# Hashes on the full TensorE array, split operands for every head, and measured durations in a list scheduler

## The chip, the core and the metric

One core of a Trainium2 chip runs the whole program. The metric is device microseconds (us) of one execution. TensorE (PE) multiplies, VectorE (DVE), ScalarE (ACT) and GpSimd (POOL) do the elementwise work, and SyncE (SP) issues the DMAs.

## The reference, cut to what matters

Three stages, one after the other, on a batch of 2 sequences of 768 tokens with 8 heads of 64:

```python
q_bits = (einsum(q, proj) > 0)            # 6 hash bits a row, the same for k
mask = q_bucket[:, :, :, None] == k_bucket[:, :, None, :]
scores = where(mask, q @ k.T / 8, -1e9)   # attention within equal buckets
x = softmax(scores) @ v                   # -> 1536 x 512
h = ((x @ w1) * (x @ w2)) @ w3 @ w_out    # inner width 1024
out = (sigmoid(h @ w_gate) * (h @ w_val)) @ w_out2   # inner width 1536
```

Weights arrive as float64 and are decoded on the chip to float32. The products must hold float32 accuracy: a float32 value is split into a float32r high part and a float32r low part, and two or three float32r products stand for one float32 product.

## The kernel before, in words

**Attention** goes through 16 heads (`h`) of 6 row tiles (`g`, 96 in all). For a tile, `emit_qk` (L465, L468) puts 128 x 768 scores into one of two PSUM tiles, `emit_max` (L474, DVE) takes the row maximum, `emit_exp` (L484, ACT) the exponentials. For two tiles together (a unit, 48 in all) `emit_T` transposes on PE (L517) in three groups of four, copies each group out of PSUM on ACT (L520), and, for heads from `PLAIN = 2` on, writes the low part on DVE (L522). `emit_av` (L535) multiplies by v. For heads 0 and 1 it is six plain float32 matmuls with 64 columns of v as weights. For the other heads it is twelve float32r matmuls with 128 weight columns (high and low part of v side by side, made by `split_v` on POOL, L375 and L376), and `emit_x` then adds the two halves with one ACT copy and one DVE addition (L548). Plain heads need the ACT copy alone.

**The mask** rides in the score matmul: 64 extra contraction rows carry a pattern of the bucket. `hashes` makes them, twice a head: three matmuls with `pq` as weights (L388), the signs on ACT (L390), one matmul with the pattern `pat` (L391); DVE compares the result with a threshold (L413). DMAs on SP then move rows between partition halves.

**A filler** multiplies w3 by w_out (L590, 8 blocks of 24 matmuls) between the attention steps, each weight tile loaded by a 512 KB DMA and decoded by ACT, POOL and DVE (L337 to L346); afterwards the first quarter of the next stage takes its place. What follows attention, with three-part products at L695, runs to the end.

**The order** in the attention part is written by `order_engines`, which plays through all instructions with a cost for each (`cost`), a latency for each pair of engines and a landing time for each DMA, picks on each engine the ready instruction of highest priority, and then fixes that order on every engine and on SP's queue. Each engine works off its list in order: a wait at its head holds what is behind it.

Of the kernel before, what the change touches and what calls it, by code (L numbers as in the profile page):

```python
# [10 lines left out]
F32 = mybir.dt.float32  # L11
F32R = mybir.dt.float32r
U32 = mybir.dt.uint32
I32 = mybir.dt.int32
# [3 lines left out]
AF = mybir.ActivationFunctionType  # L18
# [10 lines left out]
class Tiles:  # L29
# [3 lines left out]
    rings = {}  # L33
# [12 lines left out]
def order_engines(tc):  # L46
# [8 lines left out]
    rings = Tiles.rings  # L55
    N = len(ins)

    def count(x):
        n = 1
        for _, c in list(x.ap)[1:]:  # L60
            n *= c
        return n
# [12 lines left out]
    def cost(k):  # L75
        i, e, op = ins[k], eng[k], type(ins[k]).__name__
        rd = [x for x in i.ins if hasattr(x, "ap")]
        n = max([count(i.outs[0])] + [count(x) for x in rd[:1]])
        if e == "PE":
            passes = 1 if "float32r" in str(rd[0].dtype) else 2 if n == 128 else 4  # L80
            return n / 2.4 * passes + 2.5
        if e == "Activation":
            return 971 if n == 768 else 50 + n * 0.836
        if e == "Pool":
            return 60 + n * 2.3
        if e == "DVE":
            if op in ("InstTensorTensor", "InstTensorReduce") or (op == "InstTensorScalarPtr" and len(rd) > 1 and count(rd[1]) > 8):
                return 69 + n * 1.04
            return 585 if op == "InstTensorScalarPtr" and n == 384 else 69 + n * 0.52
        return 600  # L90

    step = {("Activation", "DVE"): 145, ("Activation", "PE"): 200, ("Activation", "Pool"): 170, ("DVE", "Activation"): 132,
# [53 lines left out]
    def blocked(k):  # L146
        for t in opens.get(k, ()):
            g = rings[t][0]
            if slots[g] <= 0 or queue[g][taken[g]] != t:
                return g  # L150
            if g[0] == "mw" and pools.get("wtmp"):
                return "wtmp"
        return None
# [4 lines left out]
    dma = 0.0  # L158

    def wake(g):  # L160
        for k in waiting.pop(g, ()):
            heapq.heappush(ready[eng[k]], (ins[k].bass_priority, k))

    def post(t, what, x):
        heapq.heappush(events, (t, next(tick), what, x))
# [4 lines left out]
    while events:  # L170
        now = events[0][0]
        while events and events[0][0] <= now:
            _, _, what, x = heapq.heappop(events)
            if what == "ready":
                heapq.heappush(ready[eng[x]], (ins[x].bass_priority, x))
            elif what == "slot":
                g = rings[x][0]
                slots[g] += 1
                pools[g[0]] -= 1
                wake(g)  # L180
                if not pools[g[0]]:
                    wake(g[0])
            elif what == "end":
                for u in ends[x]:
                    left[u] -= 1
                    at[u] = max(at[u], now + step.get((eng[x], eng[u]), 60))
                    if not left[u]:
                        post(at[u], "ready", u)
                for t in held.get(x, ()):
                    todo[t] -= 1  # L190
                    if not todo[t]:
                        post(now + 200, "slot", t)
        again = True
        while again:
            again = False
            for e in ranks:
                while free[e] <= now and ready[e]:
                    _, k = heapq.heappop(ready[e])
                    g = blocked(k)
                    if g is not None:  # L200
                        waiting.setdefault(g, []).append(k)
                        continue
                    for t in opens.get(k, ()):
                        g = rings[t][0]
                        slots[g] -= 1
                        taken[g] += 1
                        if slots[g] > 0 and waiting.get(g):
                            wake(g)
                            again = True
                    order[e].append(k)  # L210
                    for u in begins[k]:
                        left[u] -= 1
                        at[u] = max(at[u], now)
                        if not left[u]:
                            post(at[u], "ready", u)
                    free[e] = done = now + cost(k)
                    if e == "SP":
                        n = count(ins[k].outs[0]) * list(ins[k].outs[0].ap)[0][1] * mybir.dt.size(ins[k].outs[0].dtype)
                        dma = max(now + 1080, dma) + n / 360
                        done = dma + 900  # L220
                    post(done, "end", k)
                    post(free[e], "free", k)
# [8 lines left out]
def lsh_attention_moe_moe2_kernel(  # L231
# [20 lines left out]
    B, H, S, D = v.shape  # L252
    P = 128
    NB = proj.shape[1]
    NT = S // P
    HS = S // 2
# [13 lines left out]
    act = nc.scalar  # L270
    dve = nc.vector
    pool = nc.gpsimd
    pe = nc.tensor
    sync = nc.sync

    def act_copy(dst, src):
        act.activation(out=dst, in_=src, func=AF.Copy)  # L277
# [4 lines left out]
    cst = Tiles(ctx.enter_context(tc.tile_pool(name="cst", bufs=1, side="left")), "cst", 1)  # L282
# [3 lines left out]
    psT = Tiles(ctx.enter_context(tc.tile_pool(name="psT", bufs=4, space=bass.MemoryType.PSUM)), "psT", 4)  # L286

    idf = cst.tile([P, P], F32, name="idf")
    pq_raw = cst.tile([P, NB], F32, name="pq_raw")
    pq = [cst.tile([P, D], F32R, name=f"pq{i}") for i in range(2)]  # L290
    thr = cst.tile([P, 2], F32, name="thr")
    scl = cst.tile([P, 1], F32, name="scl")
    zb = cst.tile([D, 1], F32, name="zb")
    pat = cst.tile([D, P], F32R, name="pat")
    bits = [cst.tile([D, P], I32, name=f"bits{i}") for i in range(2)]

    xall = big.tile([P, KC, NTOK], F32, name="xall")
    xraw = [xall[:, :, i * CH:(i + 1) * CH] for i in range(NSW)]
# [4 lines left out]
    psS = Tiles(att_ctx.enter_context(tc.tile_pool(name="psS", bufs=1, space=bass.MemoryType.PSUM)), "psS", 1)  # L303
    scs = [psS.tile([P, 2, 512], F32, name=f"s{i}") for i in range(2)]
    ap_ = Tiles(att_ctx.enter_context(tc.tile_pool(name="att", bufs=2, side="right")), "att", 2)
# [40 lines left out]
        dve.tensor_tensor(out=dst.bitcast(I32), in0=ai, in1=ri, op=ALU.add)  # L346


    PLAIN = 2

    raws, splits, mats = {}, {}, {}

    def load_v(h):
        if h < NH:
            if h < PLAIN:
                t = ap_.tile([P, 2, NT, D], F32, tag="spv", name=f"spv{h}")[:, 0]
# [13 lines left out]
    def split_v(h):  # L370
        if not PLAIN <= h < NH:
            return
        t = ap_.tile([P, NT, 2, D], F32R, tag="spv", name=f"spv{h}")
        splits[h, "v"] = t
        (pool if h >= 2 else dve).tensor_copy(t[:, :, 0, :], raws[h, "v"])  # L375
        pool.tensor_tensor(out=t[:, :, 1, :], in0=raws[h, "v"], in1=f(t[:, :, 0, :]), op=ALU.subtract)  # L376
# [6 lines left out]
    def hashes(m, half):  # L383

        hs = slice(half * HS, (half + 1) * HS)
        ps = psT.tile([P, 512], F32, tag="t", name="gps")
        for n, (w, x) in enumerate(((0, "aq"), (0, "bq"), (1, "aq"))):
            pe.matmul(ps[0:D, :HS], lhsT=pq[w], rhs=m[x][:, hs], start=n == 0, stop=n == 2)  # L388
        sg = ap_.tile([D, HS], F32R, tag="sg", name="sg")
        act.activation(out=sg, in_=ps[0:D, :HS], func=AF.Sign, scale=2.0 ** 64, bias=zb)  # L390
        pe.matmul(ps[:, :HS], lhsT=pat, rhs=sg, start=True, stop=True)  # L391
        return ps

# [30 lines left out]
    def first_head():  # L424
# [19 lines left out]
        for d in ("bk", "ak"):  # L444
            pool.tensor_copy(m[d][0:D], t[1][0:D])
        act_copy(m["bk"][D:P], f(m["bq"][D:P]))
        pss = [hashes(m, half) for half in range(2)]
        act.activation(out=m["bq"][D:P], in_=t[1][D:P], func=AF.Copy, scale=SCALE)
        for d, r in (("ak", slice(0, D)), ("aq", slice(D, P))):
# [59 lines left out]
    def emit_T(g, j):  # L509

        if g % 2 == 0 and j == 0:
            n, dt = (1, F32) if g < PLAIN * NT else (2, F32R)
            pt_t[g // 2] = [ap_.tile([P, 2, NT, P], dt, tag=f"pt{i}", name=f"pt{i}_{g}") for i in range(n)]
# [12 lines left out]
    def emit_av(u):  # L526
        pts = pt_t.pop(u)
        h, t = divmod(2 * u, NT)
        sv = raws[h, "v"] if h < PLAIN else splits[h, "v"].rearrange("p c a d -> p c (a d)")
        acc = psT.tile([P, 512], F32, tag="t", name=f"av{u}")  # L530
# [7 lines left out]
    def emit_x(u):  # L538
# [4 lines left out]
        x = xall[r0:r0 + D, hh // 2, b * S + t * P:b * S + (t + 2) * P]  # L543
        if h < PLAIN:
            act_copy(x, acc[0:D, :2 * P])
# [254 lines left out]
    start = first_head()  # L800
    next(start)
    make_identity(nc, idf)
    o = D // 2
    pool.iota(bits[0], pattern=[[0, 2], [1, D]], base=0, channel_multiplier=0)
    for r in range(0, D, o):
        pool.iota(bits[1][r:r + o], pattern=[[0, P]], base=0, channel_multiplier=1)
# [85 lines left out]
    for _ in first:  # L892
        pass
    order_engines(tc)
    prio(0, 200000)
    att_ctx.close()
# [44 lines left out]
```

## Time and profile before

| | |
|---|---|
| median of 3 runs | 832.86 us (831.72 to 833.24) |
| profiled execution, its own time | 831.98 us |
| its span, first to last instruction | 830.2 us |
| PE busy | 801.8 us, 97% of the span |
| ACT, DVE, POOL busy | 513.3, 458.0, 429.5 us |
| mean granted TensorE clock | 0.992 |

The span is what the rows cover; the profiled execution's time is 1.8 us longer. A busy PE counts from the start of a matmul to its modelled end, so the step from one start to the next says more about cost than a duration does.

### The profile page before, as it was taken

To read this page: it belongs to the slowest core of one execution; us is meant where nothing else is said; L and a number is where in the kernel's file an instruction comes from. 1 tells how busy PE (TensorE), PEld (TensorE's weight loads), DVE (VectorE), ACT (ScalarE), POOL (GpSimd) and SP (SyncE) were. 2 spreads that over 40 slices of the span, in tenths; PEclk is the share of its full clock that TensorE was granted. 3 is DMA by queue.
4 is the path that set the end of the run, shared out by engine and by line. 5 is a ranking of instruction groups with operands and counts; after the bars stand their busy time and mean duration, and the time that the engine had idled before them with its cause. 6 is when DMAs were issued, how large, how long until landed. Compare 5 with 4: busy or idle time off the path is not lost.

```text
span 830.2 us, 11487 instructions
## 1 busy us (share of the span) xinstructions
PE 801.8 (97%) x4016; PEld 657.1 (79%) x4016; DVE 458.0 (55%) x696; ACT 513.3 (62%) x944; POOL 429.5 (52%) x457
## 2 busy tenths in 40 slices
PE   5899899999999999999999999999999999999998
PEld 3577688888787888887888888888888888888886
DVE  5536787777788878977354535564522222222222
ACT  5788778787788888876455655766534333343332
POOL 5567656665466555559355556677633333333330
PEclk9999899999999999999999999999999999999999
DMA  8744547454455644131022122344001000010001
GB/s 259 199 153 129 171 125 188 130 156 112 121 147 145 147 102 128 61 137 51 1 74 79 52 77 76 103 152 135 17 1 51 1 1 1 0 52 1 0 1 51
DMA packets 28585, 74.46 MB, mean 90 GB/s; under 512 B 6128, under 2 KB 8432, under 8 KB 28528
## 3 DMA queue, kind: packets, MB, share of 16 engines
q1 hardware_dynamic: 28528, 73.73, 29.9%
q8 instruction: 32, 0.52, 0.3%
q14 instruction: 25, 0.20, 0.1%
HBM read 52.83 MB, written 3.19 MB: 67 GB/s over the span
## 4 chain that ended last, share of the span: by engine, by line
PE 86%; DVE 8%; ACT 3%; issue 1%; POOL 1%; DMA 0%; SPq 0%; DVEq 0%; POOLq 0%; ACTq 0%
PE m L695 18%; PE pa L695 17%; PE pb L695 17%; PE av L535 8%; PE tp L517 6%; PE wacc L590 5%; PE p L695 4%; PE s L465 3%; PE s L468 3%; DVE sm L474 2%; PE y L695 2%; PE gps L388 2%; DVE pt L522 2%; DVE da L341 1%; PE gps L391 1%
## 5 line engine op out<-in xcount | busy, mean ns | idle before, releaser
L735 DVE TENSOR_TENSOR pb<-pb,a 128x512 f32<-128x512 f32 x52 | 36.3, 699 | 179.0 <-PE pb L695 175.6
L474 DVE TENSOR_REDUCE sm<-s 128x1 f32<-128x768 f32 x96 | 91.0, 949 | 32.2 <-PE s L468 25.2
L689 POOL TENSOR_TENSOR wal<-xall,wah 128x512 fp32r<-128x512 f32 x36 | 46.9, 1304 | 107.2 <-ACT wah L277 107.2
L517 PE MATMUL tp<-idf,e 128*128 128x128 f32 x576 | 99.8, 278 | 1.0 <-DVE pt L522 1.0
L695 PE MATMUL pa<-x,wah 128*128 128x512 f32 x320 | 99.2, 390 | 0.0
L695 PE MATMUL pb<-x,wbh 128*128 128x512 f32 x320 | 98.6, 389 | 0.0
L520 ACT ACTIVATE pt<-tp 128x512 fp32r<-128x512 f32 (+1 forms) x144 | 82.8, 597 | 23.7 <-PE tp L517 22.6
L484 ACT ACTIVATE e<-s,sm 128x768 f32<-128x768 f32 x96 | 86.6, 902 | 13.8 <-DVE sm L474 12.4
L339 POOL TENSOR_SCALAR dr<-st 128x512 bf16<-128x512 f32 x76 | 71.0, 943 | 46.4 <-issue 25.7
L522 DVE TENSOR_TENSOR pt<-tp,pt 128x512 fp32r<-128x512 f32 x126 | 83.4, 683 | 18.1 <-ACT pt L520 17.7
L535 PE MATMUL av<-pt,spv 128*128 128x256 f32 (+1 forms) x576 | 86.0, 299 | 1.3 <-DVE pt L522 1.2
L517 PEld LDWEIGHTS tp<-idf,e 128*128 128x128 f32 x576 | 72.4, 143 | 12.5 <-issue 2.4
L535 PEld LDWEIGHTS av<-pt,spv 128*128 128x128 f32 (+1 forms) x576 | 73.7, 184 | 10.7 <-DVE pt L522 2.8
L590 PE MATMUL wacc<-wo,t 128*128 128x512 f32 x192 | 70.6, 434 | 6.3 <-ACT wo L277 2.8
L695 PEld LDWEIGHTS pa<-x,wah 128*128 128x128 f32 x320 | 60.1, 188 | 13.2
L695 PEld LDWEIGHTS pb<-x,wbh 128*128 128x128 f32 x320 | 60.1, 188 | 12.6
L465 PE MATMUL s<-bk,bq 128*128 128x384 f32 x192 | 61.8, 375 | 6.2 <-ACT e L484 5.7
L340 POOL TENSOR_SCALAR da<-da 128x512 f32<-128x512 f32 x76 | 48.3, 640 | 36.6 <-ACT da L337 32.5
L695 PE MATMUL pa<-x,wal 128*128 128x512 f32 x160 | 62.4, 391 | 0.9 <-POOL wal L689 0.9
L695 PE MATMUL pb<-x,wbl 128*128 128x512 f32 x160 | 62.5, 390 | 0.0
L468 PE MATMUL s<-ak,aq 128*128 128x384 f32 x192 | 60.2, 369 | 0.0
L338 ACT ACTIVATE dr<-st 128x512 int16<-128x512 uint32 x76 | 59.9, 788 | 0.0
(143 smaller groups left out, 1810.2 us busy)
## 6 DMA issues: line engine op xcount, KB each, us to landing
st<-in_moe_w_dram SPq DMA_DIRECT2D x32, 512.0 KB, 4.3
st<-in_moe_w_out_dram SPq DMA_DIRECT2D x20, 512.0 KB, 4.3
st<-in_moe_w_gate_dram SPq DMA_DIRECT2D x12, 512.0 KB, 3.2
st<-in_moe_w_val_dram SPq DMA_DIRECT2D x12, 512.0 KB, 3.2
qk<-in_qk_dram SPq DMA_DIRECT2D x15, 384.0 KB, 4.2
rr<-row SPq DMA_DIRECT2D x16, 192.0 KB, 3.5
out_dram<-o SPq DMA_DIRECT2D x12, 256.0 KB, 2.0
ak<-aq SPq DMA_DIRECT2D x15, 192.0 KB, 2.6
```

Source lines behind the costliest of these rows:

```text
L338: act.activation(out=r.bitcast(I16)[:, 0::2], in_=lw, func=AF.Copy, scale=2.0 ** -29)
L339: pool.tensor_scalar(out=r.bitcast(BF16)[:, 1::2], in0=f(hw), scalar1=0.0, scalar2=1.0, op0=ALU.mult, op1=ALU.mult)
L465: pe.matmul(s[:, half, :HS], lhsT=m["bq"][:, qs], rhs=m["bk"][:, ks], start=True, stop=False)
L468: pe.matmul(s[:, half, :HS], lhsT=m["aq"][:, qs], rhs=m["ak"][:, ks], start=False, stop=True)
L474: dve.tensor_reduce(out=b, in_=s[:, :, :HS], op=ALU.max, axis=AX.XY, negate=True)
L484: act.activation(out=e.rearrange("p (a c) -> p a c", a=2), in_=s[:, :, :HS], func=AF.Exp, bias=sm, scale=1.0, accum_out=su_t[h][:, t:t + 1],)
L517: pe.transpose(ps[:, i * P:(i + 1) * P], e_t[g - g % 2 + a][:, c * P:(c + 1) * P], idf)
L520: act.activation(out=dh, in_=src, func=AF.Copy)
L522: dve.tensor_tensor(out=d, in0=src, in1=f(dh), op=ALU.subtract)
L535: pe.matmul(acc[:w.shape[1], :2 * P].rearrange("p (a t) -> p a t", a=2), lhsT=w, rhs=r[:, :, c], start=(c == 0 and i == 0), stop=(c == NT ...
L590: pe.matmul(acc, lhsT=t3[x][:, j], rhs=wo[y][:, j], start=(j == 0 and n == 0), stop=(j == NF1 - 1 and n == 2))
L695: mm = pe.matmul(ps, lhsT=lhs[x], rhs=rhs[y], start=start and n == 0, stop=stop and n == 2)
```

## The change

The weights `pq` of the hash matmuls go from 64 to 128 columns (the added ones are zero), so the signs cover 128 rows, and `pat` has 128 rows (the added ones are zero). The scratch tiles `bits`, used once at the start, move into the ring of `ft`. `PLAIN` becomes 0, so heads 0 and 1 are split as all others are: their v goes through the single-buffered `rawv` and `split_v`, their transposed probabilities get a low part. In `order_engines` the costs of PE, ACT, POOL and DVE instructions and of DMA landings get other numbers; every engine's order in the attention part is made anew from them.

```diff
+        banks = [x for x in rd + [i.outs[0]] if (region(x) or ("",))[0] in rings and rings[region(x)[0]][0][0] in ("psT", "psS")]
         if e == "PE":
             passes = 1 if "float32r" in str(rd[0].dtype) else 2 if n == 128 else 4
-            return n / 2.4 * passes + 2.5
+            return n / 2.4 * passes + (16 if passes == 1 else -12 if passes == 2 else 4)
         if e == "Activation":
-            return 971 if n == 768 else 50 + n * 0.836
+            return 971 if n == 768 and banks else 50 + n * (0.836 if banks else 1.0)
         if e == "Pool":
-            return 60 + n * 2.3
+            if op == "InstTensorTensor":
+                return 40 + n * 2.4 if n < 768 else 2200
+            return 100 + n * 1.15
         if e == "DVE":
+            if op == "InstCustomDveAnt":
+                return 720
             if op in ("InstTensorTensor", "InstTensorReduce") or (...):
-                return 69 + n * 1.04
-            return 585 if op == "InstTensorScalarPtr" and n == 384 else 69 + n * 0.52
+                return 69 + n * (1.04 if banks else 1.4)
+            return 585 if op == "InstTensorScalarPtr" and n == 384 else 69 + n * 0.6
...
-                        dma = max(now + 1080, dma) + n / 360
+                        dma = max(now + 1900, dma) + n / 300
                         done = dma + 900
...
-    pq = [cst.tile([P, D], F32R, name=f"pq{i}") for i in range(2)]
+    pq = [cst.tile([P, P], F32R, name=f"pq{i}") for i in range(2)]
-    zb = cst.tile([D, 1], F32, name="zb")
-    pat = cst.tile([D, P], F32R, name="pat")
-    bits = [cst.tile([D, P], I32, name=f"bits{i}") for i in range(2)]
+    zb = cst.tile([P, 1], F32, name="zb")
+    pat = cst.tile([P, P], F32R, name="pat")
...
-    PLAIN = 2
+    PLAIN = 0
...
-            pe.matmul(ps[0:D, :HS], lhsT=pq[w], rhs=m[x][:, hs], start=n == 0, stop=n == 2)
-        sg = ap_.tile([D, HS], F32R, tag="sg", name="sg")
-        act.activation(out=sg, in_=ps[0:D, :HS], func=AF.Sign, scale=2.0 ** 64, bias=zb)
+            pe.matmul(ps[:, :HS], lhsT=pq[w], rhs=m[x][:, hs], start=n == 0, stop=n == 2)
+        sg = ap_.tile([P, HS], F32R, tag="sg", name="sg")
+        act.activation(out=sg, in_=ps[:, :HS], func=AF.Sign, scale=2.0 ** 64, bias=zb)
         pe.matmul(ps[:, :HS], lhsT=pat, rhs=sg, start=True, stop=True)
...
+    bits = ap_.tile([P, S], F32R, tag="ft", name="bits", bufs=1).bitcast(I32)
+    bits = [bits[0:D, i * P:(i + 1) * P] for i in range(2)]
```

## Rows read from the trace of the kernel before

**Rows 1.** Page, busy time and instructions of each engine
```profile
PE 801.8 (97%) x4016; PEld 657.1 (79%) x4016; DVE 458.0 (55%) x696; ACT 513.3 (62%) x944; POOL 429.5 (52%) x457
```

**Rows 2.** Stretches: length, busy time by engine (instructions), granted clock, DMA
```profile
20.00:80.00 60.00, 56.14 (x292) 40.16 (x291) 32.34 (x48) 47.88 (x94) 39.11 (x48) 0.96 0.56 160
...
90.00:100.00 10.00, 8.63 (x43) 7.39 (x44) 7.09 (x11) 7.21 (x15) 7.29 (x9) 0.66 0.31 101
...
100.00:380.00 280.00, 272.69 (x1677) 233.65 (x1676) 228.02 (x341) 227.14 (x448) 167.35 (x197) 1.00 0.48 131
220.00:240.00 20.00, 17.95 (x111) 14.74 (x111) 19.23 (x30) 17.34 (x36) 11.30 (x14) 1.00 0.47 134
260.00:280.00 20.00, 19.60 (x125) 16.96 (x125) 18.97 (x30) 16.86 (x33) 12.15 (x16) 1.00 0.56 163
...
500.00:600.00 100.00, 100.00 (x432) 80.72 (x431) 54.34 (x86) 66.20 (x111) 70.01 (x70) 1.00 0.30 100
```

**Rows 3.** Waits of PE: total us, times, longest us
```profile
PE gps L388 <- ACT aq L440: 6.7, 1, 6.7
PE s L465 <- ACT e L484: 5.7, 6, 1.4
PE wacc L590 <- ACT wo L277: 2.8, 1, 2.8
PE wacc L590 <- ACT t L277: 2.5, 3, 1.4
...
PE wacc L590 <- POOL wo L585: 0.9, 1, 0.9
```

**Rows 4.** Timeline of PE, one unit of head 1 and one of head 2
```profile
62.16 2.80 PE L535 MATMUL av<-pt,spv 128*64 128x256 f32 x12
64.89 0.50 PE L590 MATMUL wacc<-wo,t 128*128 128x512 f32 x1
...
82.80 1.58 PE L535 MATMUL av<-pt,spv 128*128 128x256 f32 x12
84.21 0.27 PE L517 MATMUL tp<-idf,e 128*128 128x128 f32 x1
```

**Rows 5.** Timeline of PE around one pattern matmul of the hashes
```profile
103.00 0.34 PE L388 MATMUL gps<-aq,pq 128*64 128x384 f32 x1
103.17 0.34 PE L468 MATMUL s<-ak,aq 128*128 128x384 f32 x1
103.35 0.39 PE L590 MATMUL wacc<-wo,t 128*128 128x512 f32 x1
103.67 0.44 PE L391 MATMUL gps<-sg,pat 64*128 64x384 f32 x1
104.04 0.44 PE L517 MATMUL tp<-idf,e 128*128 128x128 f32 x2
```

**Rows 6.** Timeline of PE's weight loads, the same pattern matmul
```profile
103.67 0.18 PEld L391 LDWEIGHTS gps<-sg,pat 64*128 64x128 f32 x1 [0.30 <-ACT sg L390]
```

**Rows 7.** Line L391: duration ns least, median, most; first and last start
```profile
L391 PE MATMUL gps<-sg,pat x32: 435/439/686, 9.9 to 322.4; 64*128 64x384 f32 x32
```

**Rows 8.** Groups of instructions by form: busy us, mean ns, idle before
```profile
L522 DVE TENSOR_TENSOR pt<-tp,pt 128x512 fp32r<-128x512 f32 x126 | 83.4, 683 | 18.1 <-ACT pt L520 17.7
L520 ACT ACTIVATE pt<-tp 128x512 fp32r<-128x512 f32 x126 | 72.5, 598 | 20.9 <-PE tp L517 19.7
L339 POOL TENSOR_SCALAR dr<-st 128x512 bf16<-128x512 f32 x76 | 71.0, 943 | 46.4 <-issue 25.7 <-DVE w1r L346 10.1 <-DVE wc L346 5.6
...
L390 ACT ACTIVATE sg<-gps,zb 64x384 fp32r<-64x384 f32 x32 | 17.8, 572 | 6.1 <-PE gps L388 5.7
L548 DVE TENSOR_TENSOR xall<-av,xall 64x256 f32<-64x256 f32 x42 | 17.4, 415 | 14.2 <-ACT xall L277 13.7
...
L376 POOL TENSOR_TENSOR spv<-rawv,spv 128x384 fp32r<-128x384 f32 x14 | 15.3, 1094 | 1.0
```

**Rows 9.** DMA issues: count, KB each, median us to landing
```profile
st<-in_moe_w_dram SPq DMA_DIRECT2D x32, 512.0 KB, 4.3
```

## The prediction

> **What bounds the kernel now.** I read the page first: PE is busy 801.8 of 830.2 us, no other engine above 513.3 [rows 1]. That is an average over two parts, so the stretches come next [rows 2]. Behind attention PE never rests (500 to 600 us: 100.00 busy), and the change touches nothing there. In attention, from 100 to 380 us, PE is busy 272.69 of 280, DVE 228.02 and ACT 227.14 (81% each). So attention is bound by PE too, but with two engines not far behind. An instruction taken off PE's list there shortens the run, as long as DVE and ACT can follow. The early stretch, 20 to 80 us, has PE at 56.14 of 60 and DVE at only 32.34. The waits of PE tell what is lost now [rows 3]: 6.7 us at the start for the first load, 5.7 for exponentials, and 2.8 + 2.5 + 0.9 = 6.2 us for operands of the filler, which PE's list held too early. Last I read the timeline for the steps from start to start, because durations overlap.
>
> **Plain float32 to split for heads 0 and 1.** A unit's product with v takes 64.89 - 62.16 = 2.73 us in plain float32 and 84.21 - 82.80 = 1.41 us split [rows 4]. Two heads have 2 x 6 / 2 = 6 units, so PE loses 6 x 1.32 = 8.0 us of work. In return DVE gets 6 x 3 low parts of 0.683 us (12.3 us), 6 additions of 0.415 (2.5) and 2 copies of v. The trace has no such copy on DVE; I bound it by 0 and by the 0.683 of a wider tile, and take the upper end, 1.4. Sum 16.2 us [rows 8]. POOL gets 2 subtractions of 1.094 us, which the 60 - 39.1 us it has free from 20 to 80 us hide; without that cover they cost 2.2 [rows 2, 8]. With the 8.0 us gone from the stretch, DVE has 32.3 + 16.2 = 48.5 us to do in 52, or 93%. The two fullest DVE stretches later show what that does to PE: at 19.23 of 20 PE idled 2.05 us, at 18.97 only 0.40 [rows 2]. Scaled to 52 us this is 1 to 5 us; I take the middle, 3 us lost. What would be late is the low part, and with it the next product with v on PE, and behind the DVE's subtraction the row maxima of the next tiles.
>
> The v of head 1 now waits until `split_v` has read head 0's, because the raw tile has one buffer. That load sits on SP's queue with the weight loads behind it. A weight load lands in 4.3 us [rows 9], so a misplaced v load would hold the decode by 0 to 4.3 us, once. The new order plans for this wait, so I take 0 and keep 4.3 as the bound.
>
> **The hashes on 128 rows.** The pattern matmul has 64 rows of weights now. Its weight load does not start until its own matmul does (both 103.67), where others run ahead [rows 5, 6]. Before it, a matmul of 512 columns takes 103.67 - 103.35 = 0.32 us. The normal step of that size is 100 us / 432 = 0.23 [rows 2], so 0.09 is lost. The step after it is 104.04 - 103.67 = 0.37, where a matmul of 384 columns on the full array steps by 103.35 - 103.17 = 0.18; I use the 0.17 of the neighbour at 103.00, so 0.20 is lost. Together 0.29 us. There are 32 of them with nearly one duration (435 least, 439 median) [rows 7]. The first two run in the start, where PE waits anyway; 30 x 0.29 = 8.7 us leaves PE.
>
> The Trainium skill, TensorEngine Tiling (Array Packing), Key Properties, says that changing the tiling mode drains TensorE. For 64 rows the trace agrees (0.29 us a visit). The page makes no exception for 64 columns, and there the trace disagrees: from the last hash matmul with 64 columns to the next with 128 the step is 0.17 us, as between equals [rows 5]. By the page the sum would be rival 5's, by the rows it stays.
>
> The wider hash weights cost nothing by the same steps: 0.17 with 64 columns, 0.18 with 128 [rows 5]. If the longer load of 128 columns showed, it would be 0.01 us x 96 = 1 us. The sign over 128 rows should not be longer than over 64: the ACT copy of 128 rows and 512 elements takes 598 ns, the sign of 64 rows and 384 takes 572, so 0 to 26 ns each, 0.8 us in all of an engine that is not the bound [rows 8]. The wider constants and the `bits` move are written while PE waits 6.7 us for its first operands [rows 3]; without that cover a few memsets remain, under 0.7 us together.
>
> Of the 8.7 us, 22 visits lie between 100 and 380 us (6.4 us). DVE then has 228 us in 273.6, 83%. The stretches at 95% lost 0.4 to 2.05 in 20; at 83% I expect a trace of that, 1 us in all.
>
> **The order.** A changed number costs no instruction; it moves waits. The largest corrections: a POOL tensor-scalar of 512 elements was planned as 60 + 512 x 2.3 = 1.24 us, now 0.69, and takes 0.943 in the mean [rows 8]. A 512 KB load was planned to land after 1.08 + 1.46 + 0.9 = 3.4 us, now 1.9 + 1.75 + 0.9 = 4.5, and lands after 4.3 [rows 9]. A load planned to land 0.9 us too early is just what puts a filler matmul at the head of PE's list before its operand is there. So the gain is bounded by the 6.2 us of filler waits [rows 3] plus the clock that dropped after them: 0.66 granted from 90 to 100 us, between the levels 1.2 and 2.4 GHz, 3.4 us lost [rows 2]. In the other direction, POOL is now planned 0.25 us too short, and new waits can appear anywhere; as a bound all 8 filler blocks wait as long as the worst one, 8 x 2.8 = 22.4, less the 6.2, so 16 us more. The corrected loads are nearest to the measured waits, so I take a gain of 3, half of the filler waits.
>
> **The sum**, against the profiled execution's 831.98 us (0.9 under the median, inside the runs shown): - 8.0 + 3 - 8.7 + 1 - 3 = - 15.7, which gives 816.3. I say 816.5, about 2% faster.
>
> **Rivals.**
> 1. DVE becomes the bound in heads 0 and 1 and the whole early saving goes: 93% planned load speaks for it, the filler that PE can do meanwhile against it. With no gain of the order either: 831.98 - 8.7 = 823.3. With the v load's 4.3 us on top, 827.6.
> 2. The order gives all it can: 831.98 - 8.0 - 8.7 - 6.2 - 3.4 + 4 = 809.7, and some of the 5.7 us of waits for exponentials lies beyond that, so down to 804.
> 3. Slower: PE's list holds the first matmul of each filler block before its weight is decoded, because POOL's decode is planned too short. The waits in [rows 3] show that such a wait reaches PE. It decides from 16.7 / 8 + 6.2 / 8 = 2.9 us a block, about the worst wait of now; with the clock dropping behind half of them (4 x 3.4 = 13.6) the time is 831.98 - 16.7 + 16.2 + 13.6 = 845. Against it: POOL's error shrinks from +0.3 to -0.25 us, and loads get more time.
> 4. The gap before the pattern matmul is a wait for the sign, not for the array: the load's idle time of 0.30 ends with ACT's sign [rows 6]. Then 30 x 0.09 = 2.7 us stay: 819. The 0.20 behind it can't be the sign's.
> 5. Entering and leaving a run of 64-column matmuls costs PE what the pattern matmul costs it. With one such run for each of the 30 pattern matmuls another 30 x 0.29 = 8.7 us goes: 816.3 - 8.7 = 807.6. The step of 0.17 us at 103.00 speaks against it [rows 5]. This is the rule of the Trainium skill's TensorEngine Tiling (Array Packing), Key Properties, applied to columns.
>
> **Chances.** The forecast, 811 to 822: 0.49; rival 4 inside it: 0.06; rival 1, 822 to 829: 0.17; rival 2, 804 to 811: 0.15; rival 5: 0.02; rival 3: 0.07; and a part of rival 3 that just cancels the gains: 0.04. Under 0.2% (1.7 us) a measurement of this kernel, whose three runs lie 1.5 us apart, can't tell a difference from none. Faster 0.89, same 0.04, slower 0.07. The range 806 to 829 leaves out the 0.11 above and some 0.07 of rival 2 below.
>
> **What the profile after would show.** No form 128*64 or 64*128; the pattern matmul stepping by 0.17 to 0.18 us with its weight load ahead of it; 48 units of av with about 1.4 us each. L522 with 144 instructions, L548 with 48. PE's waits for wacc under 6.2 us. DVE near 48 us in the first 75. The stage behind attention unchanged in length, only earlier. The forecast is wrong if PE's waits in attention grow by over 10 us, above all for DVE's low parts before 80 us, or if the granted clock stays low early.

## The result and the profile after

The changed kernel takes 813.48 us (median of 4 runs, 812.90 to 815.98) against 833.05 for the kernel before: a ratio of 0.9771 (95% interval 0.9745 to 0.9797), 19.6 us faster. The forecast was 816.5 in a range of 806 to 829. The total came out near; the terms behind it did not, and they are what the experiments are about.

The page of the changed kernel, busy time and instructions of each engine (compare [rows 1]):

```profile
PE 785.3 (97%) x4016; PEld 657.4 (81%) x4016; DVE 469.1 (58%) x722; ACT 512.2 (63%) x944; POOL 436.1 (54%) x459
```

PE does 16.5 us less and DVE 11.1 more; ACT's work is unchanged. The stretches of the changed kernel (columns as in [rows 2]):

```profile
20.00:80.00 60.00, 52.70 (x330) 44.97 (x330) 51.76 (x80) 53.40 (x107) 50.84 (x63) 1.00 0.70 190
20.00:100.00 80.00, 71.46 (x446) 60.86 (x447) 70.87 (x109) 71.85 (x142) 67.30 (x83) 1.00 0.73 196
...
380.00:800.00 420.00, 420.00 (x1824) 342.10 (x1823) 157.32 (x241) 200.92 (x338) 183.27 (x165) 1.00 0.13 43
```

Of the kernel before, the early and the late stretch:

```profile
20.00:100.00 80.00, 72.47 (x378) 53.62 (x378) 48.26 (x70) 62.91 (x123) 51.82 (x64) 0.93 0.56 161
...
380.00:800.00 420.00, 420.00 (x1825) 342.15 (x1824) 163.11 (x248) 204.40 (x345) 196.50 (x175) 1.00 0.13 44
```

Read the instruction counts in brackets. From 20 to 100 us PE is busy no longer than before (71.46 against 72.47) but gets 446 matmuls done instead of 378. ACT does 142 instructions instead of 123, DVE 109 instead of 70, the DMAs move 22% more a second, and the granted clock is 1.00 instead of 0.93. From 380 to 800 us PE is full in both, with 1824 and 1825 matmuls: that part moved forward and kept its length, as forecast.

PE's waits in the changed kernel (columns as in [rows 3]):

```profile
PE wacc L594 <- ACT wo L282: 2.9, 2, 2.0
...
PE wacc L594 <- ACT t L282: 0.6, 1, 0.6
...
PE wacc L594 <- POOL wo L589: 0.3, 1, 0.3
```

The filler's waits fell from 6.2 to 2.9 + 0.6 + 0.3 = 3.8 us, a small part of 19.6. These waits can't show how much work each engine's list (its fixed order of instructions) got through, and there the two kernels differ by more.

### The profile page after: what moved, and what is told of

It is laid out like the page before. It is cut to its first block, busy times and chain, and to the rows that moved or that the text cites. A ratio compares the mean times of both kernels' runs of the same rounds, so it can differ in the third digit from the quotient of the medians.

```text
span 810.8 us, 11521 instructions
## 1 busy us (share of the span) xinstructions
PE 785.3 (97%) x4016; PEld 657.4 (81%) x4016; DVE 469.1 (58%) x722; ACT 512.2 (63%) x944; POOL 436.1 (54%) x459
## 4 chain that ended last, share of the span: by engine, by line
PE 84%; DVE 7%; ACT 5%; POOL 2%; issue 1%; DMA 1%; SPq 0%; POOLq 0%; ACTq 0%; DVEq 0%
PE m L699 18%; PE pa L699 18%; PE pb L699 18%; PE av L539 6%; PE tp L521 5%; PE p L699 5%; PE wacc L594 4%; PE s L469 3%; PE s L472 3%; PE y L699 3%; DVE pt L526 2%; PE gps L392 2%; DVE sm L478 1%; ACT e L488 1%; ACT pt L524 1%
## 5 line engine op out<-in xcount | busy, mean ns | idle before, releaser
L526 DVE TENSOR_TENSOR pt<-tp,pt 128x512 fp32r<-128x512 f32 x144 | 94.9, 681 | 11.4 <-ACT pt L524 10.7
L343 POOL TENSOR_SCALAR dr<-st 128x512 bf16<-128x512 f32 x76 | 73.0, 970 | 41.1 <-issue 21.0
L488 ACT ACTIVATE e<-s,sm 128x768 f32<-128x768 f32 x96 | 86.7, 905 | 12.3 <-DVE sm L478 11.7
L524 ACT ACTIVATE pt<-tp 128x512 fp32r<-128x512 f32 x144 | 82.5, 600 | 11.0 <-PE tp L521 9.3
L539 PE MATMUL av<-pt,spv 128*128 128x256 f32 x576 | 77.2, 283 | 1.0 <-DVE pt L526 0.9
L539 PEld LDWEIGHTS av<-pt,spv 128*128 128x128 f32 x576 | 71.5, 188 | 5.8 <-DVE pt L526 4.1
L699 PEld LDWEIGHTS pa<-x,wah 128*128 128x128 f32 x320 | 60.1, 188 | 13.2
L594 PE MATMUL wacc<-wo,t 128*128 128x512 f32 x192 | 66.7, 418 | 3.7 <-ACT wo L282 2.9
L344 POOL TENSOR_SCALAR da<-da 128x512 f32<-128x512 f32 x76 | 50.1, 665 | 31.1 <-ACT da L341 26.7
```

Source lines behind the costliest of these rows:

```text
L343: pool.tensor_scalar(out=r.bitcast(BF16)[:, 1::2], in0=f(hw), scalar1=0.0, scalar2=1.0, op0=ALU.mult, op1=ALU.mult)
L488: act.activation(out=e.rearrange("p (a c) -> p a c", a=2), in_=s[:, :, :HS], func=AF.Exp, bias=sm, scale=1.0, accum_out=su_t[h][:, t:t + 1],)
L524: act.activation(out=dh, in_=src, func=AF.Copy)
L526: dve.tensor_tensor(out=d, in0=src, in1=f(dh), op=ALU.subtract)
L539: pe.matmul(acc[:w.shape[1], :2 * P].rearrange("p (a t) -> p a t", a=2), lhsT=w, rhs=r[:, :, c], start=(c == 0 and i == 0), stop=(c == NT ...
L594: pe.matmul(acc, lhsT=t3[x][:, j], rhs=wo[y][:, j], start=(j == 0 and n == 0), stop=(j == NF1 - 1 and n == 2))
```

## The experiments

All times are medians, with the ratio to the kernel before on the same chip where one is quoted. A gain in us that stands behind a ratio is worked out from it; a difference from the changed kernel is one of medians, and under some 2 us it is within the spread of the runs. Every run makes the order anew from its own instructions, so a small part of any difference can be the order's.

### Each part alone, and two without the third

The change has three parts that can be had one by one: hashes on 128 rows and columns, split heads 0 and 1, and the new numbers in `order_engines`. `hash_only`, `split_only` and `order_only` take the kernel before with one of them.

The edits are the lines of the change itself, and all of these kernels have the move of `bits`. In `hash_only`:

```diff
-    pq = [cst.tile([P, D], F32R, name=f"pq{i}") for i in range(2)]
+    pq = [cst.tile([P, P], F32R, name=f"pq{i}") for i in range(2)]
-    pat = cst.tile([D, P], F32R, name="pat")
+    pat = cst.tile([P, P], F32R, name="pat")
...
-        sg = ap_.tile([D, HS], F32R, tag="sg", name="sg")
+        sg = ap_.tile([P, HS], F32R, tag="sg", name="sg")
```

In `split_only`:

```diff
-    PLAIN = 2
+    PLAIN = 0
```

In `order_only` all new lines of `cost`, and:

```diff
-                        dma = max(now + 1080, dma) + n / 360
+                        dma = max(now + 1900, dma) + n / 300
```

`hash_split` has the first two edits and not the third.

> The kernel before with the hashes on 128 rows and columns alone; float32 heads 0 and 1 and the old costs stay. Theory 1 (the terms of the sum hold one by one): 8.7 us less PE work, about 1 given back, so 7 to 9 us under the kernel before, near 825. Theory 2 (the new order brings most, because a gain on PE is lost in the old order's waits): under 4 us, 829 or more. The pattern matmul should step by 0.17 to 0.18 us.

825.02 us, ratio 0.9912 (0.9895 to 0.9928): 7.3 us, as the sum said. PE's busy time falls from 801.8 to 793.1 us, by just the 8.7 us of the forecast.

> The kernel before with heads 0 and 1 split alone. Theory 1: 8.0 us less PE work, 3 lost to DVE, so about 5 us under the kernel before, near 828. Theory 3 (DVE becomes the bound in heads 0 and 1): within 2 us of the kernel before, with PE waiting on DVE's low parts before 80 us. Theory 2: within 4 us.

831.37 us, ratio 0.9987 (0.9978 to 0.9997): 1.1 us, where the sum said 5. By the pages PE is busy 7.1 us less (801.8 to 794.7), and idle 5.7 us more: the work is gone, and most of it came back as idle time.

> The kernel before with the new costs of the list scheduler alone. Theory 1: 3 us under the kernel before, near 830, with under 4 us of filler waits. Theory 2: 8 us or more under it, with the granted clock at 1.0 from 10 to 50 and from 90 to 100 us, where it was 0.66 to 0.93.

818.89 us, ratio 0.9841 (0.9826 to 0.9855): 13.2 us, where the sum said 3. The new order alone is worth more than both cuts of PE's work. The granted clock is 1.00 in every ten microseconds from 10 to 100 us, where the kernel before had 0.66 to 0.93 in five of the nine.

> The changed kernel with the old costs: both cuts of PE work, old order. Theory 1: 8.7 + 8.0 - 4 = 12.7 us under the kernel before, near 820, 4 to 7 us over the changed kernel. Theory 2: over 825, more than 11 us over the changed kernel.

824.62 us, ratio 0.9907 (0.9892 to 0.9922): with the old order both cuts together bring no more than the hashes alone, and the changed kernel lies 11.1 us below. This is theory 2 for the split (its 825 missed by 0.4) and theory 1 for the hashes.

`hash_order` is the changed kernel with heads 0 and 1 in plain float32 again:

```diff
-    PLAIN = 0
+    PLAIN = 2
```

> The changed kernel with float32 heads 0 and 1 (PLAIN = 2). Theory 1: 5 us over the changed kernel, near 818. Theory 3 (DVE takes the early saving): within 2 us of the changed kernel. If the gain of the split is its whole 8.0 us of PE work: 821.5.

815.32 us: the split brings 815.32 - 813.48 = 1.8 us in the new order, which is not clear of the spread (812.63 to 816.69 here, 812.90 to 815.98 in the changed kernel).

`split_order` is the changed kernel with the hashes on 64 rows and columns again (the diff of `hash_only` turned round).

> The changed kernel with the hashes on 64 rows and columns. Theory 1: 7 to 9 us over the changed kernel, 820 to 822. Theory 2 (order brings most): under 4 us over it.

817.32 us: the hashes bring 3.8 us in the new order, half of what they bring in the old one.

### Rows or columns

`cols_only` is the changed kernel with signs and pattern on 64 rows, the hash weights staying on 128 columns:

```diff
-    pat = cst.tile([P, P], F32R, name="pat")
+    pat = cst.tile([D, P], F32R, name="pat")
...
-        sg = ap_.tile([P, HS], F32R, tag="sg", name="sg")
-        act.activation(out=sg, in_=ps[:, :HS], func=AF.Sign, scale=2.0 ** 64, bias=zb)
+        sg = ap_.tile([D, HS], F32R, tag="sg", name="sg")
+        act.activation(out=sg, in_=ps[0:D, :HS], func=AF.Sign, scale=2.0 ** 64, bias=zb)
```

> The changed kernel with 128 columns in the hash weights, but signs and pattern over 64 rows as before. If the rows alone cost PE time (my reading of the trace): the pattern matmul again steps by 0.37 us, and the time is that of the kernel with both on 64, 7 to 9 us over the changed kernel. If leaving 64 columns costs as much as leaving 64 rows: the time lies between, and the changed kernel's gain from the hashes is about twice 8.7.

817.37 us, the time of the kernel with both on 64 (817.32).

`rows_only` is the changed kernel with the hash weights on 64 columns, signs and pattern staying on 128 rows; rows 64 to 127 of two fixed sign tiles are zeroed once:

```diff
-    pq = [cst.tile([P, P], F32R, name=f"pq{i}") for i in range(2)]
+    pq = [cst.tile([P, D], F32R, name=f"pq{i}") for i in range(2)]
+    sgs = [cst.tile([P, HS], F32R, name=f"sg{i}") for i in range(2)]
...
-            pe.matmul(ps[:, :HS], lhsT=pq[w], rhs=m[x][:, hs], start=n == 0, stop=n == 2)
-        sg = ap_.tile([P, HS], F32R, tag="sg", name="sg")
-        act.activation(out=sg, in_=ps[:, :HS], func=AF.Sign, scale=2.0 ** 64, bias=zb)
+            pe.matmul(ps[0:D, :HS], lhsT=pq[w], rhs=m[x][:, hs], start=n == 0, stop=n == 2)
+        sg = sgs[half]
+        act.activation(out=sg[0:D], in_=ps[0:D, :HS], func=AF.Sign, scale=2.0 ** 64, bias=zb)
...
+    for t in sgs:
+        dve.memset(f(t[D:P]), 0.0)
```

> The changed kernel with 64 columns in the hash weights, signs and pattern over 128 rows (the upper 64 rows of two fixed sign tiles are zero, ACT writes the lower 64). If the rows alone cost PE time: within 1 us of the changed kernel, the pattern matmul at 0.17 to 0.18 us. If columns cost as well: 4 us or more over it, with steps above 0.2 us out of the last hash matmul.

813.19 us, the time of the changed kernel (813.48). So the whole gain of the hashes comes from leaving the 64 rows; no cost of the 64 columns shows. Rival 5 is out. The Trainium skill's sentence that a change of the tiling mode drains TensorE (TensorEngine Tiling (Array Packing), Key Properties) fits what the 64 rows cost here (817.37 against 813.48), and no cost of that kind shows for the 64 columns. Whether the array drains at either was not shown.

### Does DVE hold the early stretch?

Both are the changed kernel without the low parts of the probabilities of two heads; PE multiplies the high part a second time in their place. DVE loses 18 subtractions, 12.3 us by [rows 8] (by the pages it is busy 8.9 and 10.3 us less), and PE keeps its work. `no_low_early` (in `no_low_late` the heads are 8 and 9):

```diff
-            n, dt = (1, F32) if g < PLAIN * NT else (2, F32R)
+            n, dt = (1 if 0 * NT <= g < 2 * NT else 2), F32R
...
+        pts = pts * 2 if len(pts) == 1 else pts
```

> The changed kernel without the low parts of the probabilities of heads 0 and 1: 18 DVE subtractions (12.3 us) go, and PE multiplies the high part twice, so its work stays. The split brought 1 to 2 us of its 8.0 us of PE work. If DVE holds the early stretch (theory 3): 4 to 6 us under the changed kernel, 808 to 810, won before 100 us. If ACT or the loads hold it: within 1.5 us of the changed kernel.

814.92 us, ratio 0.9784 (0.9770 to 0.9799): nothing gained. Theory 3 falls for the new order. The stretch from 20 to 100 us of `hash_order`, the kernel with float32 heads 0 and 1:

```profile
20.00:100.00 80.00, 76.76 (x444) 61.37 (x444) 59.43 (x84) 71.78 (x141) 64.93 (x80) 0.98 0.69 190
```

The same stretch of `no_low_early`:

```profile
20.00:100.00 80.00, 71.38 (x441) 62.04 (x442) 60.55 (x90) 70.37 (x140) 66.11 (x83) 0.95 0.71 191
```

In the changed kernel DVE is busy 70.87 us of these 80, in `hash_order` 59.43, in `no_low_early` 60.55, and all three get the same number of instructions through: 446, 444 and 441 matmuls, 142, 141 and 140 on ACT. Taking 5.3 us of busy time off PE (76.76 to 71.46) leaves PE idle by as much; taking 10.3 us off DVE leaves DVE idle. So neither alone is what holds this stretch. ACT is at 70 to 72 of 80 us in all three, above DVE in each and above PE in the changed kernel alone.

> The same left out of heads 8 and 9 instead of 0 and 1: 12.3 us of DVE work go between 180 and 250 us, PE work stays. If relief of DVE counts only where the filler's decode crowds it (theory 3): within 1.5 us of the changed kernel. If DVE holds PE everywhere: 3 us or more under it.

812.18 us, ratio 0.9755 (0.9737 to 0.9773), some 1.3 us under the changed kernel, with overlapping intervals. Relief of 12.3 us on DVE is worth a tenth of itself there at most, and nothing early.

### Which number of the order?

`order_dma` is the changed kernel with the old costs and the new landing time, `order_pool` with all old numbers and the new cost of POOL.

The line that is new in `order_dma` beside the old order (`hash_split`):

```diff
-                        dma = max(now + 1080, dma) + n / 360
+                        dma = max(now + 1900, dma) + n / 300
```

The lines that are new in `order_pool` beside the old order:

```diff
-            return 60 + n * 2.3
+            if op == "InstTensorTensor":
+                return 40 + n * 2.4 if n < 768 else 2200
+            return 100 + n * 1.15
```

> The changed kernel with the old costs of all engines and only the new landing time of the loads. The new numbers together brought 11.1 us (824.6 to 813.5). If the late loads put the filler matmuls in the wrong place (my step): 814 to 818, and under 3 us of filler waits. If the engines' costs did it: 821 to 825.

823.97 us, ratio 0.9899 (0.9883 to 0.9916): the old order's time (824.62). The filler's waits, which the new landing time was to remove, are still there:

```profile
PE wacc L589 <- ACT wo L277: 6.2, 2, 3.3
```

> The changed kernel with all old numbers but POOL's, which are new. If POOL's doubled tensor-scalar cost put the decode too late: 814 to 818. If the loads' landing time did it: 821 to 825. If it takes both: both this run and the one with new landing times lie near 820.

813.79 us, ratio 0.9769 (0.9754 to 0.9783): the whole gain of the order, from POOL's costs alone. The stretch from 20 to 100 us of `order_dma`:

```profile
20.00:100.00 80.00, 66.18 (x388) 55.76 (x388) 59.64 (x95) 64.25 (x127) 53.92 (x67) 0.91 0.58 164
```

Of `order_pool`:

```profile
20.00:100.00 80.00, 71.54 (x433) 62.50 (x432) 68.52 (x107) 70.77 (x140) 63.91 (x79) 0.93 0.68 189
```

With POOL's old cost ACT gets 127 instructions done in these 80 us and PE 388 (126 and 389 in `hash_split`), with the new one 140 and 433. The filler needs one decode after another, and each has two POOL tensor-scalars of 512 elements. In `order_dma`, from 20 to 100 us (busy us, mean ns, idle before):

```profile
L338 POOL TENSOR_SCALAR dr<-st 128x512 bf16<-128x512 f32 x10 | 7.8, 778 | 0.4
L339 POOL TENSOR_SCALAR da<-da 128x512 f32<-128x512 f32 x10 | 6.1, 614 | 0.8
```

In `order_pool`, the same stretch:

```profile
L340 POOL TENSOR_SCALAR dr<-st 128x512 bf16<-128x512 f32 x14 | 12.4, 887 | 0.7
L341 POOL TENSOR_SCALAR da<-da 128x512 f32<-128x512 f32 x14 | 9.2, 654 | 3.2 <-ACT da L338 2.3
```

The old plan has 1.24 us for each, 2.48 a decode, and they take 0.78 + 0.61 = 1.39. The new plan has 2 x 0.69 = 1.38, and they take 0.89 + 0.65 = 1.54. All nine kernels here with the new POOL cost do 14 decodes from 20 to 100 us, and all five with the old one 10 or 11. So an order written with the new cost gets through three or four decodes more, with or without the two cuts. My reading of how: the old plan placed the decode's later steps, and the filler's matmuls behind them, further down the lists than the engines could have had them, and engines that keep to their lists had nothing to do meanwhile (ACT is busy 64.25 us there and 70.77 with the new cost). The same new lines also shorten the planned copies and scalings of 384 elements that feed attention, from 0.94 to 0.54 us; which form of POOL instruction matters was not tested.

## Why the prediction was right, and where it was not

**Plain float32 to split: mechanism right, gain mis-sized.** The step of 8.0 us less PE work held within an us: one unit of head 1 in the changed kernel takes 65.42 - 63.92 = 1.50 us (2.73 plain and 1.41 split in [rows 4]), all 48 have the form 128*128, and DVE has the 144 low parts and 48 additions that were forecast.

```profile
63.92 1.66 PE L539 MATMUL av<-pt,spv 128*128 128x256 f32 x12
65.42 0.49 PE L521 MATMUL tp<-idf,e 128*128 128x128 f32 x3
```

The term "8.0, 3 lost to DVE" gave 5 and measured 1.1 in the old order and 1.8 in the new. Rival 1 had the size (most of the early saving goes), and in the new order the wrong culprit. That DVE is loaded as planned is true (51.76 of 60 us from 20 to 80, 86%, against 93% of 52 forecast), but `no_low_early` shows that the load isn't what holds PE there. My argument scaled PE's idle time from the two stretches with the fullest DVE without asking what PE waited for: of the 2.05 us from 220 to 240, PE's waits put only 0.5 down to DVE and 1.5 to ACT. In the old order DVE may have a share: in `split_only` PE's waits for DVE before 100 us are 2.5 us and for the filler's `wo` 5.4, against none and 2.8 in the kernel before. What holds the early stretch in the new order was not settled. ACT at 90%, with 140 to 142 instructions in the four kernels of the new order shown above, speaks for ACT; the loads at 0.7 of the DMA engines could be it too. No run relieved either.

**The hashes: right in the old order, half in the new.** `hash_only` measured 7.3 us where the sum had 8.7 - 1 = 7.7. `cols_only` and `rows_only` show that it is the rows, as I read from the steps. In the new order 3.8 us are left, 3.9 under the sum. One part of what is missing is of the kind of rival 4, which I had at 2.7 us: the weight load of the pattern matmul can wait for the sign. The changed kernel's timeline of PE around two pattern matmuls:

```profile
137.21 0.44 PE L395 MATMUL gps<-sg,pat 128*128 128x384 f32 x1
137.49 0.34 PE L472 MATMUL s<-ak,aq 128*128 128x384 f32 x1
...
202.15 0.35 PE L395 MATMUL gps<-sg,pat 128*128 128x384 f32 x1
202.34 0.63 PE L594 MATMUL wacc<-wo,t 128*128 128x512 f32 x2
```

The weight loads (PEld) at the same places:

```profile
137.21 0.19 PEld L395 LDWEIGHTS gps<-sg,pat 128*128 128x128 f32 x1 [0.23 <-ACT sg L394]
...
202.06 0.19 PEld L395 LDWEIGHTS gps<-sg,pat 128*128 128x128 f32 x1 [0.17 <-ACT sg L394]
```

ACT's sign for the first of the two:

```profile
136.58 0.58 ACT L394 ACTIVATE sg<-gps,zb 128x384 fp32r<-128x384 f32 x1 [0.89 <-PE gps L392]
```

At 202 the load starts 0.09 us ahead of its matmul and the step is 0.19. At 137 the sign ends at 137.16, the load starts at 137.21 together with the matmul, and the step is 0.28: 0.1 of the 0.2 saved is spent again, though nothing about the array's mode is in the way any more. The duration of a pattern matmul tells the two cases apart, and the medians show which is more common. `hash_only`, old order (duration ns least, median, most):

```profile
L390 PE MATMUL gps<-sg,pat x32: 333/350/690, 10.4 to 316.5; 128*128 128x384 f32 x32
```

The changed kernel:

```profile
L395 PE MATMUL gps<-sg,pat x32: 331/442/689, 9.9 to 305.5; 128*128 128x384 f32 x32
```

In the old order most signs are early (median 350 ns), in the new one most are late (442). From 100 us on, the sign ends less than 0.06 us ahead of the matmul in 12 of 20 visits of the changed kernel, each with a step of 0.28 to 0.29, and in 4 of 22 of `hash_only`. So the step "the 0.20 behind it can't be the sign's" was too strong: half of it can. How the 3.9 us divide I estimate from the timelines of PE, with each visit's two steps held against the steps that the same neighbours have elsewhere (0.18, 0.23 and 0.03 us). In the old order (the kernel before against `hash_only`) the hashes save 5.9 us from 100 us on and 1.8 before, in the new one (`split_order` against the changed kernel) 4.1 and 1.9. So about 2 us of the missing are the late signs. The other 1.9 are saved before 100 us and don't show in the 3.8 measured, which fits a stretch that PE doesn't hold.

**The order: the step that failed.** I took the gain as bounded by the filler's waits and the clock's drop, 9.6 us, took 3 of it, and put it down to the landing time of the loads. It measured 13.2 alone and 11.1 on top of the other two. The loads' landing time brought nothing (`order_dma`); POOL's costs brought all (`order_pool`).

The bound was too low, because it counted one operand's waits and the clock in one slice. By the pages of the kernel before and `order_only`, PE is idle 8.6 us less (28.4 to 19.8) and, with the same instructions, busy 4.8 us less (801.8 to 797.0), at a mean granted clock of 1.000 instead of 0.992. Of the filler's waits 0.6 us are left, not half of 6.2. How much of the 4.8 us is the clock was not taken apart.

The other error is the size of POOL's. I had it off by 0.3 us in one direction and by 0.25 in the other, and dismissed it as even. But the 0.943 us of [rows 8] are a mean over the whole run, and 34 of its 76 instructions lie behind attention, which the list scheduler doesn't order; from 20 to 100 us they take 0.78. And I left out the decode's second tensor-scalar, planned at 1.24 too, which takes 0.61. So the old plan was 0.46 and 0.63 us too long, 1.1 us a decode, and the new one, by the times in `order_pool`, is 0.2 too short for the first and right for the second. It was not even here. How a plan that is too long costs so much is my reading, which no run took apart further: it holds work back that nothing brings forward again.

**The clock** fell behind idle time in the kernel before, as the forecast had it: PE is busy 7.70 of 10 us from 80 to 90 us, and the clock granted in the next ten is 0.66 [rows 2], between the levels 1.2 and 2.4 GHz.

```profile
80.00:90.00 10.00, 7.70 (x45) 6.07 (x46) 8.82 (x14) 7.82 (x16) 5.42 (x9) 0.99 0.76 222
```

But the changed kernel has a stretch with the same busy time, and its clock is 1.00 there and in the ten behind it:

```profile
30.00:40.00 10.00, 7.70 (x49) 6.31 (x47) 8.97 (x15) 6.70 (x15) 8.15 (x13) 1.00 0.99 258
```

So the same idle time went with a drop of the clock in one kernel and without one in the other.

**The total** was right by luck: the order gave 8 to 10 us more than its term, the split 3 to 4 less, the hashes 4 less in this order. With the measured parts the sum reads 13.2 (order) + 7.3 (hashes) + 1.1 (split) = 21.6 one by one, against 19.1 together by its ratio (19.6 by the medians): some 2 us of overlap.

## What to carry to other kernels

Before costing a cut of the busiest engine's work, look at the stretch in which the cut lies: where all engines rest a little and another is as full, the cut can come back as idle time. A planner's costs are worth checking against the trace before anything else, form by form and over the part that it plans: a mean over the whole run hid an error here, and POOL's corrected costs were worth more than two cuts of TensorE's work. A small matmul on half of the rows was cheaper here on the full array with zeros, and its streamed operand should be ready early enough for the weight load to run ahead.

## What the runs showed of the hardware that was not expected

A weight load whose matmul waits for its streamed operand did not run ahead here, even though the weights themselves are constant: 0.28 us a step instead of 0.17 to 0.19 for 384 columns. And a granted clock of 0.66 in one execution's slice does not decide a kernel's time by itself: the profiled execution of `order_pool` shows 0.66 between 60 and 70 us, and its runs still match the changed kernel's (813.79 against 813.48). Its four runs have mean granted clocks of 0.992 to 0.994, no higher than the kernel before, which takes 19 us longer.

```profile
60.00:70.00 10.00, 8.60 (x41) 7.81 (x40) 5.97 (x10) 6.51 (x13) 7.80 (x10) 0.66 0.44 155
```
